# Turning one more tile by a trip through DRAM and VectorE instead of TensorE, in a fused linear-attention and MLP kernel

## The chip, the cores and the metric

The kernel runs on one core of one Trainium2 chip. The metric is the device time of one execution in microseconds (us), the median of several runs. Engines are named as the profile names them: PE is TensorE (PEld its weight loads), DVE is VectorE, ACT is ScalarE, POOL is GpSimd, SP is SyncE, which issues nearly all DMAs of this kernel.

## The reference

The input `x` has 2048 tokens of 512 values. It is normalised, and two branches that read the same normalised tokens are added to it:

```python
xn = layernorm(x)
# branch A: linear attention, 32 heads of 16
q, k, v = split(xn @ wqkv)
phi = lambda t: where(t > 0, t + 1, exp(t)) + 1e-6
kv  = einsum("hsd,hse->hde", phi(k), v)      # a sum over all tokens
z   = sum over tokens of phi(k)
o   = (phi(q) @ kv) / (phi(q) . z + 1e-6)
A   = o @ wo
# branch B: an MLP of 512 -> 1376 -> 512
h = relu(xn @ w1 + b1) ** 2
B = h @ w2 + b2
out = x + A + B
```

## The kernel before

The tokens are 16 tiles of 128. A float32 product is done as three products of rounded parts: each operand is a high part (a copy in the matmul's format, made by ScalarE) and a low part (the rest, made by VectorE or POOL).

The kernel has two stages. The first one, the object of this change, goes once over the 16 tiles and accumulates `kx`, the product of every tile's normalised tokens with its `phi(k)`, in four PSUM banks. The second takes the tiles in two blocks of eight and does the query, MLP and output products. The order of every engine's instructions is the order in which the program is written (`tc.manual_schedule()`); no planner changes it. Each engine works its own list in order and waits at an instruction until what it needs is there.

A tile `i` of the first stage goes through these steps, each a function named here:

- `measure` and `roots`: mean and variance on VectorE (L230, L231), the reciprocal root on POOL (L241, L242).
- `normalise`: the tokens are written to `xp[i]`, for tiles 0 to 7 by VectorE (L264), for tiles 8 to 15 by ScalarE (L254). If the tile (or the second tile of a pair) belongs to `groups`, `regroup` issues on SyncE the write of `xp` to a DRAM tile `via` (L277) and puts four reads from there on the list `moves`; `move()` issues them later (L285) into a tile `xg`. The trip exchanges blocks of 32 tokens between groups of partitions.
- `transposed`: the tile is needed with features on partitions. For tiles with `i < NDVE` TensorE does four 128x128 transposes into a PSUM bank `pt` (`turned_pe`, L304). For the others VectorE does one stream transpose of 32x32 blocks from `xg` (`turn`, L289), which together with the trip through DRAM is a full transpose. Either way ScalarE copies the high part (`xs0h`, `xs1h`, L320) and VectorE subtracts the low part (`xs0l`, `xs1l`, L323). For tiles 0 to 7 the turned tile is also saved to DRAM (`keep_t`, L332); from PSUM ScalarE has to copy it first (L111), from VectorE's output it goes directly.
- `project`: twelve matmuls on TensorE make `pk`, the tile's keys (L365).
- `phi_k` and `parts`: relu and exponential on ScalarE (L356, L358), the join on VectorE (L360), then high and low part of the result (L111, L373).
- `tokens`: high and low part of the normalised tokens (ScalarE L111, POOL L119).
- `kx`: twelve matmuls on TensorE (L385).

In the main loop the step of tile `i` issues `move()`, then on TensorE `project(i)`, the transposes of the next tile if TensorE turns it, and `kx(i - 1)`, so the order on TensorE is projection, transposes, accumulation. A tile that VectorE turns is turned one step earlier than it is projected, or two, by

```python
        if NDVE < i + 2 < 13:
            run(*transposed(i + 2))
```

at the end of a step, except for tile `NDVE` itself, which stands at the top of the step ahead of its own; there its high part is taken between relu and exponential and its low part after the exponential (`mid` and `late` of `phi_k`). In the kernel before, `NDVE` is 5: tiles 0 to 4 are turned by TensorE, tile 5 alone makes a trip, the tiles 6 and 7, 8 and 9 and so on make trips in pairs.

SyncE's list is one queue: a DMA that waits for its data holds all behind it. At most eight of its DMAs are under way at once, since each one takes the completion semaphore of the eighth before it. In this stage the queue also loads `x` (`load_x`, L159), `ro` (the output weights, `fetch` and `piece_o`, L165), the biases `b1s` (L789, L791), `rq` (query weights), and saves the turned tiles 0 to 3 and 4 to 7 as 1 MB pieces `xsd` (L797), because tiles 8 to 15 reuse their places. Tile 8 can only be turned into its place after that.

Of the kernel before, what the change touches and what calls it, by code (L numbers as in the profile page):

```python
# [7 lines left out]
F32 = mybir.dt.float32  # L8
# [5 lines left out]
P = 128  # L14
# [4 lines left out]
def kernel(  # L19
# [36 lines left out]
    NJ = D // P  # L56
    TB = 4
# [1 line left out]
    BT = TB * P  # L59
    NF = -(-F // P)  # L60
    NPE = 2 * TB
    NDVE = NPE - 3
    WARM = 11
    NP = NF // 2
    FP = NF * P
# [7 lines left out]
    work = ctx.enter_context(tc.tile_pool(name="work", bufs=1))  # L73
# [17 lines left out]
    def two(name):  # L91
        return keep.tile([P, 2, 512], F32, name=name, tag=next_tag("x"))
# [10 lines left out]
    def gjc(ap):  # L103

        return ap.rearrange("p (j g c) -> p g j c", j=NJ, g=NJ)
# [49 lines left out]
    xr, xp, xg, tok, pk, kp = {}, {}, {}, {}, {}, {}  # L155

    def load_x(i, t):
        n = t.shape[1]
        nc.sync.dma_start(t, xf[i * P:(i + n) * P, :].rearrange("(i p) d -> p i d", i=n))  # L159
        for k in range(n):  # L160
            xr[i + k] = t[:, k]
# [61 lines left out]
    def group(*tiles):  # L223
        return tiles, *(small.tile([P, 3, k], F32, name=f"{n}{tiles[0]}", tag=n) for n, k in (("st", 6), ("mv", 2), ("y", 3)))

    def measure(g, *ks):

        tiles, st, mv, _ = g
        for k in ks or range(len(tiles)):
            nc.vector.bn_stats(st[:, k, :], xr[tiles[k]])  # L230
            nc.vector.bn_aggr(mv[:, k, :], st[:, k, :])  # L231
# [6 lines left out]
    def roots(tiles, st, mv, y):  # L238

        n = len(tiles)  # L240
        nc.gpsimd.tensor_scalar(y[:, 1, :n], mv[:, :n, 1], 1e-5, None, op0=OP.add)  # L241
        nc.gpsimd.tensor_tensor(out=y[:, 0, :n], in0=y[:, 1, :n], in1=power[:, :n], op=OP.pow)  # L242

    def normalise(tiles, st, mv, y):

        n = len(tiles)
        r, u = (y[:, k, :n] for k in range(2))
        if tiles[-1] >= NPE:

            nc.vector.scalar_tensor_tensor(u, mv[:, :n, 0], -1.0, r, op0=OP.mult, op1=OP.mult)  # L250
        later = []

        def last(i, o, src, k):
            nc.scalar.activation(o, src, AF.Identity, bias=u[:, k:k + 1], scale=r[:, k:k + 1])  # L254
            if i in groups:
                regroup(i)

        for k, i in enumerate(tiles):
            o, src = xp[i], xr[i]
            if i >= NDVE:  # L260

                o, src = o.rearrange("p g (j c) -> p g j c", j=NJ), gjc(src)
            if i < NPE:
                nc.vector.tensor_scalar(o, src, mv[:, k, 0:1], r[:, k:k + 1], op0=OP.subtract, op1=OP.mult)  # L264
                if i in groups:
                    regroup(i)
            else:
                later.append(lambda a=(i, o, src, k): last(*a))
        return later
# [12 lines left out]
    def move(n=8):  # L282
        for _ in range(n):
            if moves:
                nc.sync.dma_start(*moves.pop(0))  # L285
# [22 lines left out]
    def transposed(i, n=1):  # L308

        b, at = i // TB, slot(i)  # L310
        if i < NDVE:
            t = turned_pe(i, n)
# [12 lines left out]
        def keep_t():  # L325
            o = t[0]
            if i < NDVE:
                o = w512(f"t{i}", "p", 6).rearrange("p (j t) -> p j t", j=NJ)
# [11 lines left out]
    def ones(i):  # L340

        nc.gpsimd.memset(xp[i][:, D - 1:] if i < NDVE else xp[i][:, NJ - 1, P - 1:], 1.0)

    def tokens(i):
        tok[i] = pair(f"tok{i}")
        h, l = tok[i][:, 0], tok[i][:, 1]
        src = xp[i]
        if i >= NDVE:
            h, l, src = gjc(h), gjc(l), src.rearrange("p g (j c) -> p g j c", j=NJ)
        split(h, l, src, "act", "pool")  # L350
        if NDVE <= i + 1 < NT:
            ones(i + 1)
# [15 lines left out]
    def parts(i):  # L368

        p = kp[i]  # L370
        pk[i] = pair(f"pk{i}")
        copy("act", pk[i][:, 0], p, 1e-6)
        nc.vector.scalar_tensor_tensor(pk[i][:, 1], p, 1e-6, f32(pk[i][:, 0]), op0=OP.add, op1=OP.subtract)  # L373
# [142 lines left out]
    t, rk = two("x0"), four("rk", "r0")  # L516
# [7 lines left out]
    t = two("x2")  # L524
# [12 lines left out]
    groups = {}  # L537
    x4, x8 = four("x4", "r1"), four("x8", "r2")
    for i0 in range(0, NT, TB):
        a = first_xp[i0]  # L540
        for k in range(TB):
            xp[i0 + k] = a[:, k]
        if i0 + TB <= NDVE:
            continue
        n = TB if i0 >= NPE else TB // 2
        if i0 < NPE:
            i = i0 + TB - n - 1
            one = work.tile([P, 512], F32, name=f"xg{i}", tag="r0")
            xp[i], xg[i] = (t.rearrange("p (g n) -> p g n", g=NJ) for t in (xp[i], one))
            groups[i] = [xp[i], xg[i]]  # L550
        o = work.tile([P, n, 512], F32, name=f"xg{i0}", tag="r0" if i0 + TB == NT else "r3" if i0 >= NPE else "rc")
        for k in range(0, n, 2):
            i = i0 + TB - n + k
            u, v = (t.rearrange("p a (g c) -> p (a g c)", g=NJ) for t in (a[:, TB - n + k:][:, :2], o[:, k:k + 2]))
            groups[i + 1] = [t.rearrange("p (g n) -> p g n", g=NJ) for t in (u, v)]
            u, v = (t.rearrange("p (g i c) -> p g i c", g=NJ, i=2) for t in (u, v))
            for m in range(2):
                xp[i + m], xg[i + m] = u[:, :, m], v[:, :, m]
# [72 lines left out]
    rest(3)  # L631
    load_x(8, x8[:, :2])
    load_x(10, x8[:, 2:])
    load_x(12, two("x12"))
    load_x(14, two("x14"))
    project(2, pks[2], wk, HL)
    soon = group(4, 5)
    normalise(*fourth)
    phi_k(0, pks[0])
    measure(soon, 0)  # L640
    tokens(0)
    parts(0)
    phi_k(1, pks[1])
    tokens(1)
    measure(soon, 1)
    parts(1)
    roots(*soon)
    keep2()
# [36 lines left out]
    def fetch():  # L685
        while todo and len(held) < 3:
            held.append(todo.pop(0)())
# [97 lines left out]
    kxp = [bank(f"kx{c}", "acc") for c in range(NJ)]  # L785
    kx(0)
    for i in range(2, NT):
        if i == 5:
            nc.sync.dma_start(b1s[:, :NF - 1], b1[:(NF - 1) * P].rearrange("(f p) -> p f", p=P))  # L789
            for a, o, n in units(NF - 1):  # L790
                nc.sync.dma_start(b1s[a:a + n, NF - 1:], b1[o:o + n, None])  # L791
        move()
        if i in (4, 7):

            b = i // 7
            for u in range(2):
                nc.sync.dma_start(xsd[b][u], f32(cols(b * TB)[u]))  # L797
        fetch()
        ps = pks[i] if i < 3 else bank(f"pk{i}")
        if i > 2:  # L800
            project(i, ps, wk, HL)
        high = low = keep_t = lambda: None
        if i < NDVE:
            high, low, keep_t = transposed(i + 1)

        soon_turned = transposed(i + 2) if 11 <= i and i + 2 < NT else ()

        def mid():
            high()
            more(i)  # L810

        def late():
            low()
            more(i)

        if i == 12:
            rawz = raw_1(NF - 1)
            T.update({n: tokens_sum(n, f"B{n - 1}") for n in (1, 2)})
        if i == 12:
            w = load_1("q", 0)  # L820
        if i == 13:
            todo_1 = operands_first(0, w)
            extra.append(todo_1.pop(1))
        if i == 14:
            z = pair("w1z0")
            extra.append(lambda: split(z[:, 0], z[:, 1], rawz, "act", "dve"))
            o34 = halves(four("Tf", "r0"))
            extra.extend(sums_of(xT[NB - 1], xT[NB - 2], *o34))
            lows = [extra.pop() for k in range(2)]
            extra += [todo_1[0], lows[1], todo_1[1], lows[0], *todo_1[2:]]  # L830
        phi_k(i, ps, mid, late)
        more(i)
        run(*soon_turned)
        later = normalise(*soon) if soon else []
        parts(i)
        keep_t()
        if i == 2:
            tokens(2)
        if i + 1 < NT:
            tokens(i + 1)  # L840
        run(*later)
        if NDVE < i + 2 < 13:
            run(*transposed(i + 2))
        pieces([3, 1, 1, 2, 1][i - 11] if i > 10 else 0)
        if i == 2:
            ahead[3] = statistics(6, 7)
        if i + 2 in (4, 6, 8, 10):
            ahead[i + 2] = group(i + 6, i + 7)
        if i < 10:
            measure(ahead[(i + 2) // 2 * 2], i % 2)  # L850
        soon = ahead.get(i + 1, ())
        if soon:
            roots(*soon)
        kx(i - 1)
        more(i)
# [53 lines left out]
    for n in range(2):  # L909
        t1, t2 = NB - 1 - 2 * n, NB - 2 - 2 * n  # L910
        x1, x2 = xsb
        tag = "acc" if n else "ps"
# [60 lines left out]
        s = {}  # L973
# [60 lines left out]
        for p in range(NO + 1):  # L1034
            at_p = AT[p]
            kind, k = order[p] if p < NO else ("", 0)
            fa, fb = 2 * k, 2 * k + 1

            was, k = order[p - 1] if p else ("", 0)
# [172 lines left out]
        f = NF - 2  # L1212
# [36 lines left out]
        for e, f in enumerate(waiting[:-2]):  # L1249
# [3 lines left out]
            if e:  # L1253
                do(w2next, 2)
                if e + 8 < NF:
                    g = waiting[e + 8]
# [7 lines left out]
            if n == 0 and 1 <= e < 5:  # L1264
                k, u = divmod(e - 1, 2)
# [68 lines left out]
```

## Time and profile before

| | before |
|---|---|
| median of 3 runs | 413.56 us (413.45 to 413.88) |
| the profiled execution | 413.58 us, of which 411.9 us are its span from the first to the last instruction |
| TensorE busy | 407.2 us (99%) |
| VectorE, ScalarE, POOL busy | 311.1, 265.2, 59.0 us |
| granted TensorE clock | 1.00 |
| HBM read, written | 41.43 MB, 13.37 MB |

The rows of a timeline are the start in us from the span's start, the length, the engine, the line of the code, the operation, output and inputs by their names in the program, the shape and the count. In square brackets stands how long the engine was idle before it and what ended that. A row with several instructions runs from the first one's start to the last one's end. Rows of DMA issues (`SPq`) give the time that SyncE spent on issuing; when the data landed stands in the answers on DMA.

### The profile page before, as it was taken

The page shows a single profiled execution, that of the slowest core. Times are in us where ns is not written, and L with a number is a line of the kernel's source. Part 1 is how long each engine was busy: PE and PEld are TensorE (multiplying, and loading weights), DVE is VectorE, ACT ScalarE, POOL GpSimd, SP SyncE. Part 2 cuts the span into 40 slices and gives each one's busy share as a digit, 9 for nine tenths or more (in the row PEclk, how much of TensorE's full clock was granted, in tenths as well). Part 3 has the DMA queues.
Part 4 walks back from the last instruction along what each step waited for, and adds up shares of the span by engine and source line. Part 5 has one row for each costly group of instructions (what it writes and reads, how often), then busy time and mean ns, then how long its engine had stood idle before and what let it go on. Part 6 is the DMA issues. An engine that isn't in the chain of part 4 may idle for free.

```text
span 411.9 us, 5395 instructions
## 1 busy us (share of the span) xinstructions
PE 407.2 (99%) x1831; PEld 336.8 (82%) x1831; DVE 311.1 (76%) x555; ACT 265.2 (64%) x465; POOL 59.0 (14%) x91
## 2 busy tenths in 40 slices
PE   8999999999999999999999999999999999999996
PEld 7788888888888888888878888888888888878885
DVE  5885567797899898988449995567989686449843
ACT  4757677656678779788637631577588857737520
POOL 5542233230410000030000140100000200000210
PEclk9999999999999999999999999999999999999999
DMA  6979672810412221273366992411121880024602
GB/s 221 344 230 338 171 306 103 254 28 2 124 60 71 79 73 56 77 198 58 134 237 241 382 183 87 118 53 51 51 78 28 231 197 32 2 98 157 103 1 102
DMA packets 45661, 55.15 MB, mean 134 GB/s; under 512 B 8001, under 2 KB 29761, under 8 KB 44354
## 3 DMA queue, kind: packets, MB, share of 16 engines
q1 hardware_dynamic: 43330, 50.61, 37.3%
q0 software_dynamic: 2304, 4.20, 6.4%
q8 instruction: 14, 0.23, 0.2%
q14 instruction: 13, 0.11, 0.1%
HBM read 41.43 MB, written 13.37 MB: 133 GB/s over the span
## 4 chain that ended last, share of the span: by engine, by line
PE 98%; DMA 1%; DVE 0%; POOL 0%; issue 0%; ACT 0%
PE acc L130 37%; PE b L484 32%; PE pk L365 11%; PE kx L385 11%; PE acc L495 2%; PE pz L130 1%; PE pkv L885 1%; PE pm L130 1%; PE pz0b L130 1%; PE b L130 1%; DMA x<-in_A_x_dram 1%; PE pt L304 1%; PE acc L502 0%; PE end L130 0%; DVE st L230 0%; POOL y L242 0%
## 5 line engine op out<-in xcount | busy, mean ns | idle before, releaser
L130 PE MATMUL acc<-w2r,s 128*128 128x512 f32 x477 | 112.8, 390 | 0.0
L130 PEld LDWEIGHTS acc<-w2r,s 128*128 128x128 f32 x477 | 89.4, 188 | 19.3 <-issue 0.7
L484 PE MATMUL b<-T,aop 128*128 128x512 f32 x336 | 83.4, 389 | 0.0
L484 PEld LDWEIGHTS b<-T,aop 128*128 128x128 f32 x336 | 63.1, 188 | 13.2
L385 PE MATMUL kx<-pk,tok 128*128 128x512 f32 x192 | 46.5, 391 | 0.0
L385 PEld LDWEIGHTS kx<-pk,tok 128*128 128x128 f32 x192 | 35.8, 188 | 7.7 <-ACT pk L111 0.3
L1015 POOL DMA_DIRECT2D res<-in_B_b_dram x16 | 14.3, 1123 | 181.5 <-DVE dt L426 64.2
L484 PE MATMUL b<-xs0h,aop 128*128 128x512 f32 x112 | 36.9, 390 | 0.0
L130 PE MATMUL acc<-mh,aTsr 128*128 128x512 f32 x112 | 35.6, 389 | 0.0
L1023 DVE TENSOR_TENSOR res<-acc,res 128x512 f32<-128x512 f32 x16 | 11.0, 692 | 23.0 <-PE acc L130 18.4
L119 POOL TENSOR_TENSOR tok<-xp,tok 128x512 fp32r<-128x512 f32 x16 | 21.2, 1327 | 43.2 <-ACT tok L111 43.2
L122 DVE TENSOR_TENSOR w2r<-r,w2r 128x512 fp32r<-128x512 f32 (+2 forms) x35 | 25.6, 734 | 0.1
L484 PEld LDWEIGHTS b<-xs0h,aop 128*128 128x128 f32 x112 | 21.0, 188 | 4.4
L130 PEld LDWEIGHTS acc<-mh,aTsr 128*128 128x128 f32 x112 | 21.0, 188 | 4.4
L111 ACT ACTIVATE aop<-S 128x512 fp32r<-128x512 f32 x28 | 17.5, 623 | 11.0 <-DVE S L714 11.0
L119 DVE TENSOR_TENSOR aop<-S,aop 128x512 fp32r<-128x512 f32 x28 | 19.5, 697 | 4.8 <-ACT aop L111 4.4
L119 DVE TENSOR_TENSOR s<-c,s 128x512 fp32r<-128x512 f32 x20 | 13.6, 689 | 11.5 <-ACT s L111 11.5
L130 PE MATMUL acc<-ml,aTsr 128*128 128x512 f32 x56 | 21.8, 389 | 0.0
L484 PE MATMUL b<-xs0l,aop 128*128 128x512 f32 x56 | 21.8, 389 | 0.0
L111 ACT ACTIVATE w2r<-r 128x512 fp32r<-128x512 f32 x32 | 19.6, 619 | 2.4 <-DMA out_dram<-res 2.0
L111 ACT ACTIVATE T<-Tf 128x512 fp32r<-128x512 f32 x16 | 9.5, 624 | 16.5 <-DVE Tf L657 16.4
L484 PE MATMUL b<-xs1h,aop 128*128 128x512 f32 x56 | 19.5, 389 | 0.0
(195 smaller groups left out, 769.3 us busy)
## 6 DMA issues: line engine op xcount, KB each, us to landing
r<-in_B_w_dram SPq DMA_DIRECT2D x49, 256.0 KB, 2.9
res<-in_A_x_dram SPq DMA_DIRECT2D x8, 512.0 KB, 4.6
res<-in_B_b_dram POOLq DMA_DIRECT2D x16, 256.0 KB, 5.5
out_dram<-res SPq DMA_DIRECT2D x15, 256.0 KB, 2.1
via<-xp SPq DMA_DIRECT2D x5, 512.0 KB, 3.0
xg<-via SPq DMA_DIRECT2D x20, 128.0 KB, 2.6
xTd<-t SPq DMA_DIRECT2D x8, 256.0 KB, 4.3
x<-in_A_x_dram SPq DMA_DIRECT2D x4, 512.0 KB, 6.9
```

Of the source, the lines that this page charges most:

```text
L111: nc.scalar.activation(o, i, AF.Copy, bias=bias)
L119: ENG[el].tensor_tensor(out=l, in0=src, in1=f32(h), op=OP.subtract)
L122: nc.vector.tensor_tensor(out=l, in0=src, in1=f32(h), op=OP.subtract)
L130: nc.tensor.matmul(ps, lhsT=a[u], rhs=b[v], start=first and n == 0, stop=last and n == 2)
L304: nc.tensor.transpose(t[k][:, at:at + P], xp[i][:, j * P:(j + 1) * P], ident)
L365: nc.tensor.matmul(ps, lhsT=cols(i)[u][:, j, slot(i)], rhs=w[v][:, j, :], start=first and n == 0, stop=last and n == len(steps) - 1)
L385: nc.tensor.matmul(kxp[c], lhsT=tok[i][:, u, c * P:(c + 1) * P], rhs=pk[i][:, v], start=i == 0 and (u, v) == first, stop=i == NT - 1 and ( ...
L484: nc.tensor.matmul(ps, lhsT=a[u][:, j * P:(j + 1) * P], rhs=b[v][:, j, :], start=first and j == 0 and n == 0, stop=last and j == 1 and n == 2,
L495: nc.tensor.matmul(ps, lhsT=s[u][:, k * P:(k + 1) * P], rhs=w2s[NF - 1][u][:, a:z], start=first and u == 0, stop=stop and u == 1)
L885: nc.tensor.matmul(ps[:, at], lhsT=wvs[:, c, at], rhs=kxs[c // 2][:, c % 2, at], start=c == 0 and j == 0, stop=c == NJ - 1 and j == NJ - 1 ...
L1015: nc.gpsimd.dma_start(r[:, i], b2[None, :].partition_broadcast(P), accum_op=OP.add)
L1023: nc.vector.tensor_tensor(out=r[:, a:z], in0=ps, in1=r[:, a:z], op=OP.add)
```

## The change

`NDVE` becomes 4, so tile 4 too is turned by VectorE after a trip through DRAM; on TensorE four 128x128 transposes are left out and nothing else changes. Tiles 4 and 5 each make a trip alone (one tile `xg4s` holds both). For that tile 4 is measured, its roots are taken and it is normalised by itself, ahead of the main loop and half a step sooner than with tile 5; its `via` is written then, and its four reads are issued by `move()` at the top of the step of tile 2. Tile 5's reads stay at the top of the step of tile 3. Tile 4's stream transpose stands at the top of the step of tile 3, where TensorE's transposes stood; tile 5's moves from the top of the step of tile 4 to the end of the step of tile 3.

On SyncE the loads of tiles 12 to 15 (two of 512 KB) move from ahead of the loop to behind tile 4's reads; the first three loads of output weights from the step of tile 2 to that of tile 8; the four bias loads from the step of tile 5 to that of tile 13. ScalarE makes one copy less (tile 4 for its DRAM save). Behind the first stage no engine's order changes.

```diff
-    NDVE = NPE - 3
+    NDVE = NPE - 4
...
         if i0 < NPE:
-            i = i0 + TB - n - 1
-            one = work.tile([P, 512], F32, name=f"xg{i}", tag="r0")
-            xp[i], xg[i] = (t.rearrange("p (g n) -> p g n", g=NJ) for t in (xp[i], one))
-            groups[i] = [xp[i], xg[i]]
+            single = work.tile([P, 2, 512], F32, name=f"xg{i0}s", tag="r0")
+            for k in range(2):
+                i = i0 + k
+                xp[i], xg[i] = (t.rearrange("p (g n) -> p g n", g=NJ) for t in (xp[i], single[:, k]))
+                groups[i] = [xp[i], xg[i]]
...
     load_x(8, x8[:, :2])
     load_x(10, x8[:, 2:])
-    load_x(12, two("x12"))
-    load_x(14, two("x14"))
     project(2, pks[2], wk, HL)
-    soon = group(4, 5)
+    single = group(4)
+    soon = group(5)
     normalise(*fourth)
     phi_k(0, pks[0])
-    measure(soon, 0)
+    measure(single)
     tokens(0)
+    roots(*single)
     parts(0)
     phi_k(1, pks[1])
     tokens(1)
-    measure(soon, 1)
+    normalise(*single)
+    measure(soon)
     parts(1)
     roots(*soon)
     keep2()
...
     for i in range(2, NT):
-        if i == 5:
+        if i == 13:
             nc.sync.dma_start(b1s[:, :NF - 1], b1[:(NF - 1) * P].rearrange("(f p) -> p f", p=P))
             for a, o, n in units(NF - 1):
                 nc.sync.dma_start(b1s[a:a + n, NF - 1:], b1[o:o + n, None])
         move()
+        if i == 2:
+            load_x(12, two("x12"))
+            load_x(14, two("x14"))
...
-        fetch()
+        if i >= 8:
+            fetch()
```

## The prediction

> **What bounds the kernel now.** I read the page's busy times first, then its chain, then TensorE's timeline over the changed stage (tiles 3 to 8), then the queues that feed it.
>
> ```profile
> PE 407.2 (99%) x1831; PEld 336.8 (82%) x1831; DVE 311.1 (76%) x555; ACT 265.2 (64%) x465; POOL 59.0 (14%) x91
> ...
> PE 98%; DMA 1%; DVE 0%; POOL 0%; issue 0%; ACT 0%
> ```
>
> TensorE is the bound, in this stage too: work taken from it shortens the run, work given to others costs nothing until it makes TensorE wait. Here are TensorE's rows in time: start, length, engine, line, output and inputs, count.
>
> ```profile
> 24.05 1.07 PE L365 MATMUL pk<-wkh,xs1l 128*128 128x512 f32 x4
> 24.96 0.60 PE L304 MATMUL pt<-ident,xp 128*128 128x128 f32 x4
> 25.31 3.02 PE L385 MATMUL kx<-pk,tok 128*128 128x512 f32 x12
> 28.17 0.39 PE L365 MATMUL pk<-wkh,xs0h 128*128 128x512 f32 x1
> ...
> 30.89 2.88 PE L385 MATMUL kx<-pk,tok 128*128 128x512 f32 x12
> 33.61 0.39 PE L365 MATMUL pk<-wkh,xs0h 128*128 128x512 f32 x1
> ...
> 39.05 0.39 PE L365 MATMUL pk<-wkh,xs0h 128*128 128x512 f32 x1
> ...
> 49.93 0.39 PE L365 MATMUL pk<-wkh,xs1h 128*128 128x512 f32 x1
> ```
>
> Each `kx` group is an accumulation for a tile, each first `pk` row the start of the next tile's projection: tile 4 at 28.17, tile 5 at 33.61, tile 6 at 39.05, tile 8 at 49.93. No row shows a wait. So these starts are the due times of everything below.
>
> **The gain: four transposes leave TensorE.** From the start of tile 4's transposes to tile 4's projection are 28.17 - 24.96 = 3.21 us. A `kx` group with nothing before it takes 33.61 - 30.89 = 2.72 us. So the transposes and what they disturb cost 3.21 - 2.72 = 0.49 us, and every later due time moves 0.49 earlier: tile 4 to 27.68, tile 5 to 33.12, `kx` of tile 4 (2.72 after tile 5's start) to 35.84, tile 6 to 38.56, tile 8 to 49.44.
>
> ```profile
> L304 PE MATMUL pt<-ident,xp x20: 270/272/330, 5.9 to 25.3; 128*128 128x128 f32 x20
> ```
>
> One transpose lasts 0.272 us, but they overlap their neighbours, so 4 x 0.272 = 1.09 is not what is saved. [...]
>
> **What replaces them, tile 4.** VectorE turns 32x32 blocks after a trip through DRAM: write `via`, four `xg` reads, one stream transpose. The rows that price it, SyncE first:
>
> ```profile
> 11.36 3.91 SPq L159 DMA_DIRECT2D x<-in_A_x_dram  x4
> ...
> 19.76 2.21 SPq L165 DMA_DIRECT2D ro<-in_A_wo_dram  x3
> 22.54 0.33 SPq L277 DMA_DIRECT2D via<-xp  x1
> ...
> 26.55 1.75 SPq L285 DMA_DIRECT2D xg<-via  x4
> ...
> 33.12 0.43 SPq L797 DMA_DIRECT2D xsd0h<-xs1h  x1
> 33.59 0.43 SPq L797 DMA_DIRECT2D xsd0l<-xs1l  x1
> ...
> 36.15 0.33 SPq L277 DMA_DIRECT2D via<-xp  x1
> ...
> 42.97 1.79 SPq L285 DMA_DIRECT2D xg<-via  x4
> ```
>
> Times to landing of single issues (bytes, us), in order: tile 5's `via`, the last `xg` reads of tile 5, the `via` of tiles 6 and 7, the two 1 MB saves, the `via` of tiles 8 and 9 (issued at 36.15); last the median of the 20 reads of two-tile groups.
>
> ```profile
> via<-xp SPq DMA_DIRECT2D x1, 256.0 KB, 4.0
> ...
> xg<-via SPq DMA_DIRECT2D x2, 64.0 KB, 2.0
> ...
> via<-xp SPq DMA_DIRECT2D x1, 512.0 KB, 2.8
> ...
> xsd0h<-xs1h SPq DMA_DIRECT2D x1, 1024.0 KB, 4.5
> xsd0l<-xs1l SPq DMA_DIRECT2D x1, 1024.0 KB, 7.2
> ...
> via<-xp SPq DMA_DIRECT2D x1, 512.0 KB, 6.5
> ...
> xg<-via SPq DMA_DIRECT2D x20, 128.0 KB, 2.6
> ```
>
> VectorE's rows, the last two its stream transposes of tiles 5 and 8:
>
> ```profile
> 17.32 0.69 DVE L360 SCALAR_TENSOR_TENSOR k<-pk,k 128x512 f32<-128x512 f32 x1 [0.34 <-ACT k L358]
> ...
> 21.52 0.99 DVE L264 TENSOR_SCALAR xp<-x,mv,y 128x512 f32<-128x512 f32 x2
> ...
> 25.34 0.18 DVE L231 BATCH_NORM_AGGREGATE mv<-st 128x2 f32<-128x6 f32 x1
> ...
> 28.99 0.69 DVE L230 BATCH_NORM_STATS2 st<-x 128x6 f32<-128x512 f32 x1
> ...
> 29.92 0.71 DVE L289 STREAM_TRANSPOSE t<-xg 128x512 f32<-128x512 f32 x1
> ...
> 47.32 0.71 DVE L289 STREAM_TRANSPOSE xT<-xg 128x512 f32<-128x512 f32 x1 [1.98 <-DMA xg<-via]
> ```
>
> The new normalisation of tile 4 follows the VectorE instruction at 17.32 and takes half of 0.99: it ends near 18.5. VectorE does the same number of normalisations, one only earlier, so what follows it moves by half a microsecond at most, then is level. The new `via` lands between 2.8 (twice the bytes, quiet queues) and 4.0 us later (behind three weight loads). Two of the four `x` loads at 11.36 and all `ro` loads are gone from this stretch, so I take 3.0: 21.5. The four reads then occupy SyncE for 1.75; the last starts 1.3 in and lands 2.0 later: 24.8. VectorE gets to the transpose after the aggregate at 25.34, so the trip is covered with 0.7 to spare. Turn (0.71) and ScalarE's copy (0.62, below) bring tile 4's high part to 26.8, due 27.68. Cost nothing; cover 0.9; if the trip takes 1.6 us more, each further microsecond is a stall. VectorE gains 0.71 of work, ScalarE loses the copy that it made of tile 4 for its DRAM save; neither is the bound.
>
> On POOL tile 4's roots now run between the token parts of tiles 0 and 1, where POOL was idle for 1.46 us:
>
> ```profile
> 17.88 1.29 POOL L119 TENSOR_TENSOR tok<-xp,tok 128x512 fp32r<-128x512 f32 x1 [1.46 <-ACT tok L111]
> ```
>
> ScalarE's prices, tile 5's high part first:
>
> ```profile
> 31.58 0.62 ACT L320 ACTIVATE xs0h<-t 128x512 fp32r<-128x512 f32 x1
> ...
> 33.56 0.63 ACT L111 ACTIVATE pk<-k 128x512 fp32r<-128x512 f32 x1 [0.84 <-DVE k L360]
> ...
> 34.62 1.51 ACT L254 ACTIVATE xp<-x,y 128x512 f32<-128x512 f32 x2
> ...
> 48.07 0.63 ACT L320 ACTIVATE xs1h<-xT 128x512 fp32r<-128x512 f32 x1 [1.51 <-DVE xT L289]
> ```
>
> **Tile 5 pays.** On SyncE its `via` (22.54 before) now stands behind tile 4's reads and behind the loads of tiles 12 to 15, which the change puts between. Reads issued until 23.3, the two loads at 23.3 and 23.75, `via` at 24.2. The loads are 1 MB: like `xsd0h`, 4.5 us, landing at 27.8. The `via` moves behind them: a second MB cost `xsd0l` 33.59 + 7.2 - (33.12 + 4.5) = 3.2 us, so 256 KB cost 0.8: 28.6. Reads from 28.6, last landing at 28.6 + 1.3 + 2.0 = 31.9. Before, VectorE turned tile 5 at 29.92; now it waits for that until 31.9, 2.0 later. Behind it on VectorE stand tile 5's low part, the statistics and tile 4's `k` and `pk`; on ScalarE the high part stands ahead of tile 4's relu and exponential (before, the relu went first). High part ready: 31.9 + 0.71 + 0.62 and some 0.07 of handing over = 33.3, due 33.12: a stall of 0.2. Then tile 4's `pk`: relu and exponential, 1.2 by twice the 31.58 row's length, to 34.5; VectorE meanwhile does the low part (two inputs, 0.69 like `k`) and the statistics (0.69 + 0.18) until 34.9, then `k` (0.69) to 35.5; ScalarE's `pk` (0.63) to 36.2, due 35.84. The stalls are not added, as the first moves the later due time: 0.35 in all. Tile 6 follows: its `via` goes after tile 5's reads, at 28.6 + 1.75 = 30.35, and lands 2.8 later at 33.2; SyncE has by then passed tile 5's DRAM save, which waits for the turned tile (32.6). The reads' last landing is 1.3 + 2.6 later, 37.1, turned at 37.8. ScalarE, from 36.2, makes tile 5's tokens (0.6), the normalisations of tiles 8 and 9 (1.51) and then this high part: 38.8, due 38.56 + 0.35. It just fits.
>
> Bounds: if tile 4's `via` lands after 2.8 and tile 5's no later than the loads ahead of it (27.6), tile 5 lands near 30.9 and nothing stalls. If something holds tile 5's `via` up by what its 4.0 row has over 2.8 and then its reads by the 0.4 that tile 4's could lose (4.0 against my 3.0 allows up to 1.0), it is 1.6 more: stall near 1.9. I take the middle, as the queue ahead is counted in.
>
> [...] The rows decide; the sum stands at 0.35.
>
> **The moved loads.**
>
> ```profile
> 39.46 3.40 SPq L791 DMA_DIRECT2D b1s<-in_B_b_dram  x3
> ...
> 78.31 3.77 SPq L700 DMA_DIRECT2D rq<-in_A_wqkv_dram  x2
> 100.44 0.31 SPq L871 DMA_DIRECT2D zd<-zrow  x1
> ```
>
> Biases now follow `rq` at 82.1; their SyncE time is some 5 us (the 3.40 and a first one that I put at half of it), before the next SyncE item at 100.44. Nothing. The `ro` loads go to the step of tile 8, and the first piece of them is split only in that of tile 11, three steps of 5.44 us later. Nothing. In their old place the biases held SyncE until 42.97; freeing it brings little, since the `via` of tiles 8 and 9 landed at 36.15 + 6.5 = 42.65, behind the 2 MB of `xsd0`. Those now leave after tile 6's reads, at 33.2 + 1.75 = 35.0 instead of 33.12, and push that `via` 1.9 later, less 0.8 for tile 4's save (256 KB), which no longer stands between: 43.7. The reads begin 0.7 after 42.97, and tile 8's high part, 48.07 + 0.63 before, comes to 49.4, due 49.44 + 0.35: no further stall, cover 0.4.
>
> **Sum**, against the profiled execution (413.58 us, its span 411.9; the median of the runs shown is 413.56, so the same): -0.49 + 0.35 = -0.14, 413.4 us. About 0.2% (0.83 us) is what a measurement of this kernel can tell from no change; the forecast is no measurable change.
>
> **The rivals.**
> - Clean gain: tile 5 lands by 31.5 and TensorE never waits. For it: the quiet `via` row and that loads are removed from 11 to 23 us. 413.56 - 0.49 = 413.1. Chance 0.24.
> - Slower, tile 5's trip sets the pace: stall above 0.49 + 0.83 = 1.32, which needs its reads to land after 32.9. Place: VectorE's transpose of tile 5, TensorE idle ahead of tile 5's projection. For it: `via` took 4.0 where 2.8 was possible, and 1 MB is now directly ahead of it. Against: that takes a delay on top of the queue I have counted. With 1.6 more: 413.56 - 0.49 + 1.95 = 415.0. Chance 0.24.
> - Slower through tile 8 alone: its reads slip 1.5 more behind the saves, its high part comes at 50.9, stall 1.45 against 49.44, 414.5. VectorE waited there already (1.98). Chance 0.08.
> - The transposes occupy TensorE for their whole length: gain 1.09, 412.5. For it the 0.272 row, against it the 0.35 us from 24.96 to 25.31 for four. Chance 0.03. [...]
>
> **How the numbers follow.** The forecast (stall 0.1 to 1.3) has 0.41. With the clean gain that is 0.65 within 0.2%; slower 0.08 + 0.24 = 0.32; faster 0.03. The range goes from the clean gain with the scatter of the runs, 412.9, to just under the full late trip, 414.9; left out are the last rival and the tail of the second.
>
> **What would show it.** Right: no `pt` rows after 20 us; TensorE 0.5 us earlier at tile 4's projection; the transpose of tile 5 starting near 32 with a wait for `xg`; a TensorE gap of a few tenths before tile 5's projection or tile 4's `kx`, none later. Wrong: tile 4's transpose waiting past 26.3; a gap over 1.3 us; any gap at tile 8; or no wait of VectorE at tile 5.

## The result, and the profile after

| | before | after |
|---|---|---|
| median of 6 runs each | 413.72 us (413.45 to 414.80) | 418.03 us (417.58 to 418.85) |
| ratio | | 1.0092, 95% interval 1.0075 to 1.011 |
| the profiled execution | 413.58 us, span 411.9 | 418.47 us, span 416.8 |
| mean granted TensorE clock | 1.00 | 0.996 |

The change made the kernel slower: by 4.3 us (1.0%) from median to median, by 0.9% in the ratio over all the runs, whose interval lies above 1 as a whole. The forecast was 413.4 us and no measurable change, its range 412.9 to 414.9. The time is outside it.

The page of the changed kernel, its busy line and its chain by engine:

```profile
PE 409.1 (98%) x1827; PEld 337.7 (81%) x1827; DVE 312.7 (75%) x556; ACT 264.5 (63%) x464; POOL 59.2 (14%) x93
...
PE 92%; DMA 3%; DVE 2%; ACT 1%; POOL 1%; issue 0%; SPq 0%; DVEq 0%
```

TensorE does four instructions less and is busy 1.9 us longer, and the chain of work that ended last, which was 98% TensorE, now goes 3% through DMA and 2% through VectorE. So two things are to be looked for: a wait, and matmuls that take longer. TensorE's timeline shows both (start, length, engine, line, operation; in brackets the idle time before it and what ended that):

```profile
25.35 2.88 PE L385 MATMUL kx<-pk,tok 128*128 128x512 f32 x12
28.07 0.44 PE L365 MATMUL pk<-wkh,xs0h 128*128 128x512 f32 x1
...
30.88 2.88 PE L385 MATMUL kx<-pk,tok 128*128 128x512 f32 x12
36.52 0.50 PE L365 MATMUL pk<-wkh,xs0h 128*128 128x512 f32 x1 [2.75 <-ACT xs0h L320]
...
39.22 1.91 PE L365 MATMUL pk<-wkh,xs0l 128*128 128x512 f32 x4
40.92 3.00 PE L385 MATMUL kx<-pk,tok 128*128 128x512 f32 x12
```

Tile 4's projection follows the `kx` row ahead of it after 28.07 - 25.35 = 2.72 us: the transposes and the 0.49 us that they cost are gone. Tile 5's projection, due 2.72 after 30.88, at 33.60, starts at 36.52, 2.92 late, and waits for ScalarE's high part. Then the projection lasts 40.92 - 36.52 = 4.40 instead of 2.72: 1.68 more. Tile 6's step is 0.12 longer than two times 2.72; behind that each half of a step takes its 2.72 again, and the lateness of 2.92 + 1.68 + 0.12 = 4.7 us stays to the end of the stage. The clock of these steps, from the table of windows (window, its length, the busy times with counts of TensorE, its weight loads, VectorE, ScalarE and POOL, then the granted TensorE clock, DMA share, GB/s):

```profile
37.00:38.00 1.00, 1.00 (x6) 0.76 (x5) 0.96 (x4) 0.61 (x1) 0.00 (x0) 0.81 1.01 286
38.00:41.00 3.00, 3.00 (x9) 2.33 (x8) 1.44 (x4) 2.36 (x4) 2.08 (x3) 0.50 0.94 276
41.00:42.00 1.00, 1.00 (x6) 0.81 (x5) 0.21 (x1) 0.20 (x1) 0.18 (x2) 0.98 1.03 434
```

After the gap the clock was 0.50 for some 3.4 us: 0.38 of the first window, the whole second, little of the third.

Why tile 5 was late is read backwards from VectorE, then SyncE. VectorE's timeline, and the POOL row beside its second line:

```profile
17.68 0.69 DVE L360 SCALAR_TENSOR_TENSOR k<-pk,k 128x512 f32<-128x512 f32 x1 [0.17 <-ACT k L358]
18.29 1.54 DVE L264 TENSOR_SCALAR xp<-x,mv,y 128x512 f32<-128x512 f32 x1
...
22.33 0.54 DVE L264 TENSOR_SCALAR xp<-x,mv,y 128x512 f32<-128x512 f32 x1
...
26.58 0.71 DVE L289 STREAM_TRANSPOSE t<-xg4s 128x512 f32<-128x512 f32 x1 [0.37 <-DMA xg4s<-via]
...
35.09 0.71 DVE L289 STREAM_TRANSPOSE t<-xg4s 128x512 f32<-128x512 f32 x1 [4.29 <-DMA xg4s<-via]
```

```profile
18.24 1.30 POOL L119 TENSOR_TENSOR tok<-xp,tok 128x512 fp32r<-128x512 f32 x1
```

The 17.68 row stood at 17.32 before: this execution began 0.36 later, before anything of the change runs. Tile 4's normalisation took 1.54 us, tile 5's, the same instruction on the same shape, 0.54. In the first case POOL was making tile 1's low token part. Tile 5's turn waited 4.29 for its reads. SyncE's timeline:

```profile
19.85 0.34 SPq L277 DMA_DIRECT2D via<-xp  x1
...
23.09 1.76 SPq L285 DMA_DIRECT2D xg4s<-via  x4
24.89 0.94 SPq L159 DMA_DIRECT2D x<-in_A_x_dram  x2
25.88 0.47 SPq L277 DMA_DIRECT2D via<-xp  x1
...
31.63 1.76 SPq L285 DMA_DIRECT2D xg4s<-via  x4
```

And the times to landing (bytes, median us) of tile 4's `via`, and of the second `x` load and tile 5's `via`:

```profile
via<-xp SPq DMA_DIRECT2D x1, 256.0 KB, 3.2
...
x<-in_A_x_dram SPq DMA_DIRECT2D x1, 512.0 KB, 5.6
via<-xp SPq DMA_DIRECT2D x1, 256.0 KB, 5.7
```

Tile 5's `via` was issued at 25.88, behind 1 MB of loads issued a microsecond before, and its reads could only be issued at 31.63.

### The profile page after: what moved, and what is told of

It is laid out like the page before. It is cut to its first block, busy times and chain, and to the rows that moved or that the text cites. A ratio compares the mean times of both kernels' runs of the same rounds, so it can differ in the third digit from the quotient of the medians.

```text
span 416.8 us, 5402 instructions
## 1 busy us (share of the span) xinstructions
PE 409.1 (98%) x1827; PEld 337.7 (81%) x1827; DVE 312.7 (75%) x556; ACT 264.5 (63%) x464; POOL 59.2 (14%) x93
## 4 chain that ended last, share of the span: by engine, by line
PE 92%; DMA 3%; DVE 2%; ACT 1%; POOL 1%; issue 0%; SPq 0%; DVEq 0%
PE acc L130 37%; PE b L484 32%; PE pk L365 9%; PE kx L385 8%; PE acc L495 2%; DMA via<-xp 1%; PE pz L130 1%; PE pkv L891 1%; DVE st L230 1%; DMA x<-in_A_x_dram 1%; PE pm L130 1%; PE pz0b L130 1%; PE b L130 1%; DVE xp L264 1%; DMA xg4s<-via 0%
```

## The experiments

The theory after this reading, called P or Q in the expectations where it comes in parts: tile 5's trip is late for two reasons that add, the slow normalisation of tile 4 ahead of it and the `x` loads directly ahead of its `via`; the clock then adds to the gap. Rivals: the moved loads cost as such; removing one cause uncovers another trip that is as late; the half clock hides later waits and costs nothing. Every ratio is against the kernel before, on the same chip in the same sitting (medians 413.74 to 413.94 us).

| run | edit, against the change unless said | median us | ratio, 95% interval | TensorE gaps in its profile, from tile 4 on |
|---|---|---|---|---|
| e4_loads_alone | kernel before, with the moved loads only | 413.79 | 0.9999 (0.9988 to 1.0011) | none |
| e2_low_on_dve | normalisation kept clear of POOL | 416.28 | 1.0057 (1.0043 to 1.0071) | tiles 5, 6: 0.98, 0.70 |
| e1_x_late | `x` loads in steps 5 and 6 | 418.26 | 1.0098 (1.0067 to 1.0129) | tiles 6, 12: 0.51, 2.19 |
| e3_filler | TensorE kept busy in the gap | 417.67 | 1.0091 (1.0076 to 1.0107) | filled; tile 6: 0.43 |
| e8_ro_late_only | output weights from step 10 | 417.93 | 1.0100 (1.0084 to 1.0116) | tile 5: 2.17 |
| e5_x_ro_late | e1 and output weights from step 10 | 414.27 | 1.0013 (1.0003 to 1.0022) | tile 6: 0.45 |
| e6_all_clear | e2's edit, `x` loads behind `via`, output weights from step 10 | 415.28 | 1.0028 (1.0015 to 1.0042) | tile 6: 1.25 |
| e7_pool_again | e6 without e2's edit | 415.61 | 1.0042 (1.0030 to 1.0054) | tile 6: 1.11 |
| e9_best_56 | e5 and e2's edit | 414.35 | 1.0008 (0.9999 to 1.0018) | none above 0.25 |
| e10_best_67 | e9 with `x` loads in steps 6 and 7 | 415.40 | 1.0032 (1.0019 to 1.0044) | tiles 8, 12, 13: 0.29, 0.17, 0.38 |
| e11_saves_behind | e5, two saves put behind tile 6's reads | 415.61 | 1.0044 (1.0032 to 1.0056) | tile 8: 0.23, then 0.86 |
| e12_scalar_norm | e11, tile 4 normalised by ScalarE | 416.39 | 1.0071 (1.0056 to 1.0087) | 0.96 before tile 4; tiles 6, 8: 0.16, 0.23 |

**The moved loads alone (e4_loads_alone).** The kernel before, with `NDVE` as it was, and only these lines of the change:

```diff
-    load_x(12, two("x12"))
-    load_x(14, two("x14"))
...
-        if i == 5:
+        if i == 13:
...
+        if i == 2:
+            load_x(12, two("x12"))
+            load_x(14, two("x14"))
...
-        fetch()
+        if i >= 8:
+            fetch()
```

> The kernel before with the moved loads alone (tiles 12 to 15 at the step of tile 2, output weights from that of tile 8, biases at that of tile 13); tile 4 stays on TensorE. Theory Q: 1 MB of x instead of 0.75 MB of weights stands ahead of tile 5's via, it lands up to 2 us later, which tile 5's cover of some 1.4 us nearly hides: 413.5 to 414.5. Rival L (the moved loads are the loss by themselves, wherever tile 4 is turned): 416 or more.

413.79 us against 413.74: nothing. The moved loads do no harm by themselves. VectorE's turn of tile 5 waits for its reads there too, but by less than TensorE's slack:

```profile
30.46 0.71 DVE L289 STREAM_TRANSPOSE t<-xg 128x512 f32<-128x512 f32 x1 [0.69 <-DMA xg<-via]
```

Here too the loads stand directly ahead of tile 5's `via`, which took 4.6 us. But they were issued from 19.64 on and the `via` at 22.39, while in the change they wait until tile 4's reads are out (24.89) and the `via` follows at 25.88. So the loads are only a loss together with the second lone trip.

**The slow normalisation (e2_low_on_dve).** Tile 1's low token part goes to VectorE, behind tile 4's normalisation, so that POOL is idle then:

```diff
-        split(h, l, src, "act", "pool")
+        split(h, l, src, "act", "dve" if i == 1 else "pool")
...
-    tokens(1)
     normalise(*single)
+    tokens(1)
```

> The change with one edit: tile 1's low token part is made by VectorE, behind tile 4's normalisation, instead of by POOL beside it. Theory P (the normalisation took 1.54 instead of 0.54 us because POOL's token part ran beside it): it takes about 0.55, via of tile 4 leaves 1.0 us earlier, all of the chain to tile 5 moves 1.0, the gap of 2.75 goes to 1.7; 417.0 if the clock still halves behind it, near 415 if the shorter gap leaves it at 1.00. Rival (the length had another cause, or the loads set the chain alone): normalisation over 1.2 us, or the gap unchanged, 418.

1.75 us faster than the change's 418.03. VectorE and TensorE in its timeline:

```profile
17.93 0.55 DVE L264 TENSOR_SCALAR xp<-x,mv,y 128x512 f32<-128x512 f32 x1
```

```profile
34.26 0.50 PE L365 MATMUL pk<-wkh,xs0h 128*128 128x512 f32 x1 [0.98 <-ACT xs0h L320]
...
40.80 0.50 PE L365 MATMUL pk<-wkh,xs0h 128*128 128x512 f32 x1 [0.70 <-ACT xs0h L320]
```

The normalisation takes 0.55 again, so POOL's instruction beside it was what cost the microsecond. Tile 5's wait falls from 2.75 to 0.98, by more than that microsecond: tile 4's `via` also landed sooner, after 2.4 us instead of 3.2. The DMA behind it, a save, was issued 0.67 us after it; in the change 0.44.

```profile
via<-xp SPq DMA_DIRECT2D x1, 256.0 KB, 2.4
```

The clock stays up:

```profile
36.00:38.00 2.00, 2.00 (x10) 1.55 (x9) 1.15 (x3) 1.63 (x3) 1.19 (x3) 1.00 0.99 254
```

Tile 6's trip, which is issued behind tile 5's reads, is late next.

**The loads ahead of tile 5's `via` (e1_x_late).**

```diff
-        if i == 2:
+        if i == 5:
             load_x(12, two("x12"))
+        if i == 6:
             load_x(14, two("x14"))
```

> The change with one edit: the loads of tiles 12 and 14 no longer stand on SyncE between tile 4's reads and tile 5's via, but behind the reads in the steps of tiles 5 and 6. Theory Q (tile 5's via waits in the DMA queues behind 1 MB): via is issued near 25 and lands some 3 us later instead of 5.7, tile 5 is turned near 31.5, TensorE has no gap before tile 5's projection, the clock stays 1.00, and the transposes' 0.49 us are left as a gain: 413.0 to 413.4, against 413.7 before. Theory S (the two trips in a row on SyncE, each waited for, are what is late): the gap stays over 1.5 us, 415 to 417.

Tile 5's gap is gone: its `via` was issued at 24.64 and its reads at 26.83, 2.2 us later instead of 5.7. But the time did not fall, since two other trips came late (TensorE, then SyncE, then the landing of the `via` of tiles 12 and 13, then the clock):

```profile
39.71 0.50 PE L365 MATMUL pk<-wkh,xs0h 128*128 128x512 f32 x1 [0.51 <-ACT xs0h L320]
...
74.91 0.50 PE L365 MATMUL pk<-wkh,xs0h 128*128 128x512 f32 x1 [2.19 <-ACT xs0h L320]
```

```profile
24.64 0.38 SPq L277 DMA_DIRECT2D via<-xp  x1
...
26.83 1.73 SPq L285 DMA_DIRECT2D xg4s<-via  x4
...
57.94 4.32 SPq L165 DMA_DIRECT2D ro<-in_A_wo_dram  x3
62.36 0.75 SPq L277 DMA_DIRECT2D via<-xp  x1
```

```profile
via<-xp SPq DMA_DIRECT2D x1, 512.0 KB, 6.4
```

```profile
75.00:79.00 4.00, 4.00 (x11) 3.15 (x12) 3.56 (x6) 3.74 (x8) 0.96 (x1) 0.57 0.74 199
```

The `via` of tiles 12 and 13 stands behind two 1 MB saves and the three `ro` loads, which the change had put into step 8. Its tokens were ready when ScalarE's normalisation ended, at 57.87 + 1.50 = 59.37:

```profile
57.87 1.50 ACT L254 ACTIVATE xp<-x,y 128x512 f32<-128x512 f32 x2
```

SyncE spent 4.32 us on issuing the `ro` loads, until 62.26, so the `via` left 3.0 us after its tokens were ready. Then it took 6.4 us, TensorE waited 2.19 at tile 12, and half clock followed again. The runs scatter more here (415.81 to 420.55), and the two with a mean clock of 1.000 are the two shortest (415.81 and 416.23).

**Is it the clock? (e3_filler).** Twelve matmuls into the bank that tile 5's projection then starts anew, so that TensorE doesn't idle:

```diff
+        if i == 5:
+            for n in range(12):
+                nc.tensor.matmul(ps, lhsT=cols(4)[0][:, n % 4, slot(4)], rhs=wk[0][:, n % 4, :], start=True, stop=True)
```

> The change with 12 more matmuls (2.72 us) on TensorE ahead of tile 5's projection, into the bank that the projection then starts afresh; they use operands that are there, so they fill the gap and delay nothing. Theory C (the idle gap halves the clock, and tile 5's projection and more run at half speed for 1.9 us): granted clock 1.00 throughout, projection 2.72 instead of 4.6 us, 416.0 to 416.6. Rival (the lower clock has nothing to do with the gap, or is not paid): 417.6 to 418.5.

```profile
33.68 2.88 PE L808 MATMUL pk<-wkh,xs0h 128*128 128x512 f32 x12
36.72 0.50 PE L365 MATMUL pk<-wkh,xs0h 128*128 128x512 f32 x1 [0.16 <-ACT xs0h L320]
...
39.59 2.96 PE L385 MATMUL kx<-pk,tok 128*128 128x512 f32 x12
42.98 0.50 PE L365 MATMUL pk<-wkh,xs0h 128*128 128x512 f32 x1 [0.43 <-ACT xs0h L320]
```

The projection behind the filler takes 39.59 - 36.72 = 2.87, not 4.40, and the granted clock was 1.00 from 36.00 to 45.00: no half clock. But the total fell by only 0.36, not by the 1.4 to 2 expected. Tile 6 now waits 0.43, and up to tile 9 the steps are longer than 5.44 by 1.25 us in all, in the change by 0.12. The slow matmuls had mostly filled time in which TensorE would have waited for the next late trips. The runs of the change say the same: two of its six had a mean clock of 1.000, and took 417.58 and 418.04.

**The output weights (e8_ro_late_only, e5_x_ro_late).** `if i >= 8: fetch()` becomes

```diff
-        if i >= 8:
+        if i >= 10:
             fetch()
```

in the change itself (e8), and in e1 (e5).

> The change with one edit: output weights from the step of tile 10 on. Theory (in the change itself tile 12's late trip is hidden, since TensorE is already over 4 us late from tile 5): no difference, 417.6 to 418.5. Rival (it costs there too): 416 or less.

> The kernel with the loads of tiles 12 and 14 in the steps of tiles 5 and 6, and now the first output weights loaded from the step of tile 10 on, not 8. Theory R (tile 12's via waited behind the two 1 MB saves and 0.75 MB of output weights, and that alone made the gap and the half clock in the step of tile 12): no gap at tile 12, clock 1.00, only the half microsecond at tile 6 is left: 413.5 to 414.6. Rival (the loads of tiles 12 and 14, which now push the next via and with it the saves, are enough for it): a gap of over 1 us at tile 12 stays, 416 or more.

In the change it does nothing: 417.93. There TensorE runs 4.7 us late when tile 12 comes, which covers that trip. In e1 it takes off 4 us, 418.26 to 414.27. The `via` of tiles 12 and 13 now leaves at 59.03, 3.3 sooner than in e1. It takes 6.4 us here too, so what it gains over e1 is the earlier issue, not a faster landing (SyncE, then the landing, in e5):

```profile
59.03 0.33 SPq L277 DMA_DIRECT2D via<-xp  x1
```

```profile
via<-xp SPq DMA_DIRECT2D x1, 512.0 KB, 6.4
```

With the loads of `x` and `ro` both put elsewhere, one gap is left, at tile 6, whose `via` took 3.6 us (2.8 before) with the saves of tiles 4 and 5 right behind it:

```profile
39.05 0.50 PE L365 MATMUL pk<-wkh,xs0h 128*128 128x512 f32 x1 [0.45 <-ACT xs0h L320]
```

```profile
via<-xp SPq DMA_DIRECT2D x1, 512.0 KB, 3.6
```

It starts at 39.05, when 35.72 (the start of `kx` ahead of it) + 2.72 = 38.44 was due: 0.61 late, a little more than the 0.49 that the change saves. e5 is still 0.13% slower than the kernel before.

**All causes at once (e6_all_clear, e7_pool_again).** e6 is e2's edit, `ro` from step 10, and the `x` loads close behind a `via` instead of ahead of it: `load_x(12)` behind tile 5's `via` in step 2, `load_x(14)` behind tile 6's `via` and the saves at the end of step 3. e7 is the same without e2's edit.

> The change with three edits: tile 1's low token part on VectorE behind tile 4's normalisation; each load of x (tiles 12 and 13, then 14 and 15) issued behind the next via and the saves, where SyncE waits for that via anyway; output weights from the step of tile 10. Theory (the loss is nothing but what stands ahead of the via writes, and the gain is the 0.49 us of the four transposes): no TensorE gap after tile 3, every start 0.49 earlier, 413.1 to 413.4 against 413.7. Rival (a trip for each of tiles 4 and 5 doesn't fit on SyncE in any order): a gap over 0.5 us at tile 5 or 6, 414.5 or more.

> The kernel e6_all_clear with tile 1's low token part on POOL again. Theory P: tile 4's normalisation takes 1.5 us again and the chain is 1.0 later; with the loads out of the way tile 5 still comes in time and tile 6 just about not: 413.3 to 414.5. Rival (the collision with POOL is as large a cost as the loads): 415 or more.

Both missed. Tile 5 was in time in both, but now tile 6 wasn't. SyncE in e6, the landing of the four reads at 32.90, and TensorE:

```profile
31.51 0.68 SPq L159 DMA_DIRECT2D x<-in_A_x_dram  x1
32.90 1.75 SPq L285 DMA_DIRECT2D xg<-via  x4
```

```profile
xg<-via SPq DMA_DIRECT2D x4, 128.0 KB, 5.1
```

```profile
40.55 0.50 PE L365 MATMUL pk<-wkh,xs0h 128*128 128x512 f32 x1 [1.25 <-ACT xs0h L320]
```

A load behind the `via` is ahead of the reads: they took 5.1 us instead of 2.6. That e7 is hardly longer (the intervals overlap) fits that the microsecond of the normalisation is on the path only where tile 5 is. It doesn't show it, since tile 6's `via` landed after 2.7 us in e7 and after 3.2 in e6, which hides half a microsecond.

**Looking for a gain (e9_best_56, e10_best_67, e11_saves_behind, e12_scalar_norm).** e9 is e5 with e2's edit. e10 has the `x` loads in steps 6 and 7. e11 is e5 with the saves of tiles 4 and 5 kept in a list and issued behind tile 6's reads. e12 is e11 with tile 4 normalised by ScalarE.

> The change, with the three remedies together that earlier runs tried in parts: tile 1's low part on VectorE and tile 4's normalisation before it; the loads of tiles 12 and 14 in steps 5 and 6; output weights from step 10. Theory R (each delay has its own cause and they add): the normalisation takes 0.55 us again instead of 1.54, so tile 4's, tile 5's and tile 6's trips all start about 1 us sooner than in e5_x_ro_late; tile 6's gap there of 0.4 to 0.6 us closes, TensorE has no gap over 0.2 us up to tile 15, its clock stays at 1.00, and of the 0.49 us of saved transposes most is kept: 413.1 to 413.6, ratio 0.9985 to 0.9997 against before. Rival U: the low part on VectorE delays VectorE's other work ahead of tile 5 (measuring, rounding of tile 1) as much as it saves, or another trip comes late: gap of 0.3 us or more at tile 5, 6 or 8, 413.8 to 414.6.

> As e9_best_56, with the loads of tiles 12 and 14 one step later still, in steps 6 and 7. Theory R: tile 6's trip has no load near it, so no gap at tile 6; tile 12's trip (its measurement and its via write come at step 10 and 11) still has its x in time: 413.1 to 413.6, within 0.2 us of e9_best_56. Rival V: the load of tile 12 or 14 now stands ahead of a trip of tile 7 to 10, or comes too late for the measuring of the pair 12 and 13: a gap of 0.3 us or more behind step 7 that e9_best_56 doesn't have, 413.8 to 415.

> e5_x_ro_late, and in addition the two DRAM saves of the turned tiles 4 and 5, which stood on SyncE between the via of tiles 6 and 7 and its reads, are issued behind these reads. Theory W (tile 6's gap is the queue again): with nothing behind it that via lands in 2.8 us as in the kernel before (3.65 in e5_x_ro_late), the reads and the turn of tile 6 come 0.8 sooner, the gap of 0.6 closes, no gap over 0.2 us anywhere in the stage, and the whole saving of 0.49 us is seen: 413.2 to 413.7, ratio 0.9985 to 0.9998. Rival X (a DMA that is issued behind another doesn't slow it; the via takes 3.6 because of its own size or place): gap unchanged, 414.1 to 414.5; or the two saves, now ahead of the via of tiles 8 and 9, bring a gap at tile 8.

> e11_saves_behind, and in addition tile 4's normalisation is done by ScalarE, which takes 0.75 us (half of the 1.51 of its pairs) and doesn't share anything with POOL by theory, instead of VectorE's 1.54 beside POOL's token part. Theory P (VectorE and POOL slow each other down, ScalarE isn't in it): the normalisation takes 0.75 to 0.8 us although POOL's token part of tile 1 still runs in that time, tile 4's via leaves about 0.7 us sooner, VectorE has 1.5 us less to do there; the time is that of e11_saves_behind or up to 0.3 us less. Rival Y: ScalarE's order pays (tile 3's high part behind it comes 0.75 later): a gap of 0.2 to 0.5 us at tile 3 or 4, and the time is that much longer.

None beats the kernel before, and e9, e10 and e11 miss the 413.1 to 413.7 that their theories expected. e9 has the gaps at tiles 5 and 6 closed, and from tile 4's projection to the end of the stage TensorE still needs 73.88 us instead of 73.44, in slips of a few hundredths to 0.22 us at tiles 6 and 13: the 0.49 is eaten in small pieces. It is no faster than e5 (414.35 and 414.27). Its ratio allows at most a gain of 0.01%. In e10 the measuring of tile 12 waits 1.33 us for its `x`, so rival V holds. In e11, with no save behind it, tile 6's `via` takes 3.1 us and tile 6's projection starts 0.04 late, as theory W has it. But e12 has the same order on SyncE and shows 3.6 again, and e6 and e7, with the two saves and a load behind it, 3.2 and 2.7. So theory W is not shown, and why this write takes from 2.7 to 3.7 us (e1) stays open. In e11 the saves and the loads behind them are later by about a microsecond, and tile 12's `x` with them (VectorE's statistics of tile 12, then TensorE):

```profile
51.98 0.69 DVE L230 BATCH_NORM_STATS2 st<-x 128x6 f32<-128x512 f32 x1 [1.05 <-DMA x<-in_A_x_dram]
```

```profile
54.18 3.06 PE L387 MATMUL kx<-pk,tok 128*128 128x512 f32 x12 [0.86 <-ACT pk L111]
```

e12 doesn't tell theory P apart: the normalisation began only when POOL's instruction was over, because VectorE's small instruction ahead of it, on one number per partition, was held up itself. VectorE and POOL in e12, the third row the same instruction on two numbers with POOL idle:

```profile
17.92 1.25 DVE L250 SCALAR_TENSOR_TENSOR y<-mv,y 128x1 f32<-128x1 f32 x1
...
35.31 0.16 DVE L250 SCALAR_TENSOR_TENSOR y<-mv,y 128x2 f32<-128x2 f32 x1 [0.58 <-POOL y L242]
```

```profile
17.87 1.29 POOL L119 TENSOR_TENSOR tok<-xp,tok 128x512 fp32r<-128x512 f32 x1
```

It ended at 17.92 + 1.25 = 19.17, POOL's at 17.87 + 1.29 = 19.16. ScalarE's copy of `pk` behind it came late, and TensorE waited 0.96 us for it at its `kx` at 20.59, behind tile 3's transposes: rival Y, and at twice the price expected.

## Why the prediction was wrong

The step that failed is tile 5's trip: the prediction put its stall at 0.2 us, 0.35 with what follows at tile 4's `pk`, and it was 2.92. Two terms of that trip were too small, tile 4's normalisation ahead of it and the landing of tile 5's `via` behind the loads, and a term for the clock was missing.

- **The gain** was right: 3.21 became 2.72 in the change, 0.49 us.
- **Tile 4's trip, "takes half of 0.99"** was wrong: 1.54. The rows quoted for POOL showed it at work then (17.88 to 19.17 in the kernel before), and the prediction asked whether POOL was free for the roots and not what POOL does to VectorE beside it. The normalisation ended at 19.83 instead of 18.5, of which 0.36 is the later start of this execution and 0.97 the step's error. "Covered with 0.7" became a wait of 0.37 on VectorE; TensorE didn't wait at tile 4. VectorE's rows in the kernel before, beside the POOL row at 17.88, already had the price:

```profile
17.92 0.68 DVE L230 BATCH_NORM_STATS2 st<-x 128x6 f32<-128x512 f32 x1
...
18.74 0.98 DVE L373 SCALAR_TENSOR_TENSOR pk<-k,pk 128x512 fp32r<-128x512 f32 x1
...
22.43 0.68 DVE L373 SCALAR_TENSOR_TENSOR pk<-k,pk 128x512 fp32r<-128x512 f32 x1
```

The statistics took their usual time beside POOL; the low part of `pk` took 0.98 us beside it and 0.68 later, when POOL was idle.

- **Tile 5's `via`, "issued 24.2, landing 28.6"** was wrong twice: issued at 25.88, for the reasons above, 0.2 more for tile 4's `via` and the rest in handing over; and landed after 5.7 us instead of 4.4. The 1 MB ahead of it was priced by the save's 4.5; the second `x` load, issued about half a microsecond behind the first, took 5.6 itself. Together 3.0 late, and tile 5's projection followed: 2.92 late against the forecast of 0.2. e2 and e1 show each share by its removal: 1.75 us of the time, and the whole gap at tile 5. The first contains tile 4's `via` too, which landed after 2.4 us in e2.
- **No term for the clock.** 1.68 us in the profile, and no word on it. e3 puts its net price in the change at 0.36, because the trips behind were late as well. In e1 it was probably more, as the two runs without it were the shortest.
- **"It just fits" at tile 6** was wrong by 0.6 even where tile 5 is in time: e5 waits there. The landing of tile 6's `via`, forecast for 33.2, came at 33.24 in e5, but by luck: it was issued at 29.64 instead of 30.35, and took 3.6 us instead of the 2.8 of the quiet row. Too small was the way from there: the reads started at 33.31 and the turn at 37.62, 4.31 us later instead of 3.9, and the high part was ready at 39.00 (38.8 forecast). And the 0.35 of lateness from tile 5, which the forecast counted in tile 6's favour, was not there in e5, whose TensorE was 0.12 us ahead of the forecast's times.
- **`ro` to step 8, "Nothing"** was wrong, though it does not show in the change: e1 against e5, 4 us, and e8 shows that the change hides it. The working asked only when the weights are needed, and not which `via` stood behind them, nor how long SyncE would be held by issuing them (4.32 us in e1).
- **Biases, and tile 8, "no further stall"** were right (e4, and no gap at tile 8 in e5).
- **The rivals.** "Tile 5's trip sets the pace" (0.24, 415.0) was the mechanism, place and sign included, and its condition (reads landing after 32.9) was met: they landed shortly before the turn at 35.09. Its price had 1.6 of further delay where 3.0 came, and no clock. The forecast leaned on "that takes a delay on top of the queue I have counted". There was one, the normalisation, and the queue itself took longer than counted. Of the prediction's own signs of being wrong two came: tile 4's transpose waited past 26.3 (it started at 26.58), and a gap was over 1.3 us.

The sum by measured terms, for the profiled execution: 413.58 - 0.49 + 2.92 + 1.68 + 0.2 (tiles 4 and 6) + 0.4 (later start) = 418.3, against 418.47. It describes the path of that one execution: by e3, without the 1.68 of the clock the later trips would have taken most of its place.

## What to carry to other kernels

Before moving an instruction to another place, look at what the other engines run at that time there, and price it by a row with the same neighbour, not by its own row. For a transfer on a queue in which each item is needed, write down for every DMA that is moved which write and which reads stand behind it, check the ones after the next one too, and count the time for which issuing holds the queue: here each load that was taken from one trip made another one late, and no order of them that was tried kept the 0.49 us. When a gap disappears and the time doesn't, the next wait on the same chain has taken its place; a longer look down the same chain costs less than the next edit.

## What the runs showed of the hardware

- VectorE was held up while POOL ran a two-input instruction: 1.54 instead of 0.54 us for the normalisation of 128x512, which ended 0.3 us after POOL's (19.83 against 19.54), and in e12 1.25 us for one number per partition (0.16 for two numbers with POOL idle), ending with POOL's. A fixed share of the rate would not cost a tiny instruction a microsecond (an estimate: 1.54 / 0.54 = 2.9 times 0.16 is 0.5 us). Not every instruction was: the statistics took 0.68 beside POOL as elsewhere. ScalarE's normalisations of 128x512 took 0.80 to 0.81 us in the change, where each pair began less than 0.2 us before the same instruction of POOL, and 0.81 in e12 with POOL idle. What holds VectorE up no run here shows.
- After a gap of 2.75 us TensorE ran at a clock of 0.50 for about 3.4 us (the change). After 2.19 us in e1 the clock was 0.57 as the mean of 4 us, as much as 3.4 us at 0.50; after 2.17 us in e8 the projection took 4.44 instead of 2.72 us. After 0.98 us in e2 the clock was 1.00, and after 1.25 us in e6 the projection took 2.86 us. Two of the change's six runs show a mean clock of 1.000, the others 0.995 to 0.998; why, no run here shows.
- Transfers on SyncE's queue took longer with others ahead of them. Tile 5's `via` took 5.7 us behind 1 MB of loads, and its reads followed after 2.2 us where these were gone (e1). The four 128 KB reads took 2.6 us as the median of the kernel before, and 5.1 and 4.7 behind 512 KB of loads (e6, e7). An earlier transfer seems to be slowed by a later one: tile 4's 256 KB `via` took 2.2 to 2.5 us in the five profiles in which the next DMA was issued 0.67 us or more behind it (e2, e6, e9, e10, e12), and 2.7 to 3.3 in the seven in which it was issued 0.44 or 0.45 behind. Tile 6's 512 KB `via` doesn't show it (above).
